# Eight of sixty-four gradient stores cut into pieces by rows, on two DMA queues

## The chip, the cores and the metric

The kernel runs on one core of a Trainium2 chip. Its time is the device time of that core in microseconds, as the median of several executions. Each execution is classed fast or slow (slow: over 1.5% above the fastest of the same kernel). The core has five engines that compute or issue (PE, DVE = VectorE, ACT = ScalarE, POOL = GpSimd, SP = SyncE) and 16 DMA engines, which move data between the chip's main memory (HBM) and the core's on-chip buffer (SBUF, 128 partitions). In the profile, SyncE's and ScalarE's transfers run on queues named hardware_dynamic, GpSimd's on one named software_dynamic.

## The reference

One decode step of attention beside a gated MLP, forward and backward. Only its sizes matter here: the K and V caches are 32 heads x 8192 x 128 in bf16, both are read, and the gradient of both is written.

```python
def _A_ref(x, k_cache, v_cache, wq, wo):
    ...
    scores = jnp.einsum("bhqd,bhkd->bhqk", q, k) * (Dh ** -0.5)
    p = _softmax(scores, axis=-1)
    o = jnp.einsum("bhqk,bhkd->bhqd", p, v)
    ...
_out0, _vjp = jax.vjp(_f, A_x, A_k_cache, A_v_cache, A_wq, A_wo, B_w1, B_w3, B_w2)
_grads = _vjp(grad_out)
```

That is 64 loads and 64 stores of 2 MB each, 268 of the 304 MB that the kernel moves.

## The kernel before

Each head of K or V is one tile of 128 partitions x 8192 elements: a row of 16 KB in each partition. The gradient overwrites the tile in place (`outer`), one store writes it out, and only then does a later load reuse the tile. All of these transfers go by SyncE, in program order.

```python
    kc = A_k_cache.rearrange("b h (p j) d -> (b h) p (j d)", p=P)      # P = 128
    dvc = out_3.rearrange("b h (p j) d -> (b h) p (j d)", p=P)
    ...
    def fifo(out_, in_):
        nc.sync.dma_start(out_, in_)
    ...
    def load_next():
        if not pending or len(free_slots) < lag[0]:
            return
        kind, h = pending.pop(0)
        t = free_slots.pop(0)
        fifo(t[:], (kc if kind == "K" else vc)[h])
        kv_tiles[(kind, h)] = t
    ...
    def store(kind, h):
        t = kv_tiles.pop((kind, h))
        if kind == "K":
            hd.pop(h)
        fifo((dkc if kind == "K" else dvc)[h], t[:])
        free_slots.append(t)
        load_next()
    ...
    def outers_a(h):
        outer_v(h, 0, J // 2)
        outer_v(h, J // 2, J)
        store("V", h)
        outer_k(h, 0, J // 2)
    ...
    # the last four small stores: 3, 2, 4 and 1 rows of 256 B
    for dst, r0, cuts in ((out_0, 0, (0, 3, 5)), (out_1, NC, (0, 4, 5))):
        for lo, hi in zip(cuts, cuts[1:]):
            nc.scalar.dma_start(...[lo:hi, :], fin_bf[r0 + lo:r0 + hi, :])
```

GpSimd's queue carries only weight traffic (`nc.gpsimd.dma_start` of pieces of 80 KB to 1.9 MB).

## Time and profile before

| | before |
|---|---|
| median | 737.14 us (736.62 to 739.97, the 3 runs taken before the prediction) |
| profiled span | 735.9 us |
| PE / DVE / ACT / POOL busy | 87 / 61 / 55 / 4% |
| one 16 KB row on a DMA engine, median and mean (packet records) | 611 and 620 ns |

From the page of the kernel before: the DMA busy share in 40 equal slices of the span (9 is 90% or more), what was moved in each, and the queues (q1 is SyncE's, q0 GpSimd's).

```profile
span 735.9 us, 14854 instructions
...
DMA  9999999999999999999999999999999999999993
GB/s 338 401 409 421 425 430 423 391 413 410 428 420 423 428 427 426 417 426 428 430 417 425 430 427 426 419 431 425 427 419 427 428 428 429 425 429 429 424 391 150
...
q1 hardware_dynamic: 21328, 276.39, 89.3%
q0 software_dynamic: 5728, 26.30, 8.9%
```

The table by windows of the kernel before; the last three columns are PE's granted clock, the DMA share and GB/s.

```profile
core 0: us, PE busy (x) PEld busy (x) DVE busy (x) ACT busy (x) POOL busy (x), PEclk, DMA share, GB/s
...
260.00:700.00 440.00, 410.47 (x3891) 295.45 (x3891) 277.16 (x424) 261.57 (x533) 15.55 (x19) 0.94 1.01 426
```

The DMA engines are full, and they move 426 GB/s. That is what bounds the kernel: 303.97 MB in rows of 16 KB per 611 ns on 16 engines is about 709 us.

SyncE's waits in the kernel before (what it waited for: us in total, times, longest).

```profile
SPq L101 <- DMA out_dram<-kv: 364.1, 44, 16.8
SPq L101 <- DVE kv L430: 174.0, 26, 11.0
...
SPq L822 <- DMA out_dram<-fin_bf: 11.6, 1, 11.6
SPq L822 <- DMA out_dram<-wq_g: 9.1, 1, 9.1
```

And the timeline near the end of the kernel before: the last gradient work on DVE, the last K store, the last small stores (start, duration).

```profile
707.98 4.49 DVE L430 TENSOR_TENSOR kv<-qd,U 128x4096 bf16<-128x4096 bf16 x2
...
712.50 0.33 SPq L101 DMA_DIRECT2D out_dram<-kv  x1
...
723.38 1.43 ACTq L796 DMA_DIRECT2D out_dram<-fin_bf  x4
```

The last work on DVE ends at 723.4 us, the last small stores are issued by 724.8, and the span ends at 735.9. The packet records of the trace (one record for each packet: queue, size, start, duration; no engine number) show that all DMA engines but one are done 8.4 us before the last packet. In those 8.4 us one engine works alone. On SyncE's queue each of the 137 transfers raises its counter 16 times (2192 completion packets of 4 B), and the gap between the last raise and the one before it grows from 0.2 to 1.2 us (transfers landing at 280 to 320 us) to 3.2 to 5.3 (480 to 520), 6.0 to 6.5 (640 to 680) and 8.2 to 8.4 us (707 to 717). One engine falls behind steadily.

### The profile page before, as it was taken

The page shows a single profiled execution, that of the slowest core. Times are in us where ns is not written, and L with a number is a line of the kernel's source. Part 1 is how long each engine was busy: PE and PEld are TensorE (multiplying, and loading weights), DVE is VectorE, ACT ScalarE, POOL GpSimd, SP SyncE. Part 2 cuts the span into 40 slices and gives each one's busy share as a digit, 9 for nine tenths or more (in the row PEclk, how much of TensorE's full clock was granted, in tenths as well). Part 3 has the DMA queues.
Part 4 walks back from the last instruction along what each step waited for, and adds up shares of the span by engine and source line. Part 5 has one row for each costly group of instructions (what it writes and reads, how often), then busy time and mean ns, then how long its engine had stood idle before and what let it go on. Part 6 is the DMA issues. An engine that isn't in the chain of part 4 may idle for free.

```text
span 735.9 us, 14854 instructions
## 1 busy us (share of the span) xinstructions
PE 639.8 (87%) x6143; PEld 464.7 (63%) x6143; DVE 446.7 (61%) x745; ACT 402.5 (55%) x796; POOL 29.9 (4%) x45
## 2 busy tenths in 40 slices
PE   1999679999999999999999999999999999989950
PEld 1667457676667666766666666766666666666630
DVE  4057765666556666667656656676666655566482
ACT  1660646565656565665565655666565556655610
POOL 0010010000000000000000000000000000000000
PEclk9995799998999999999999999999999999989965
DMA  9999999999999999999999999999999999999993
GB/s 338 401 409 421 425 430 423 391 413 410 428 420 423 428 427 426 417 426 428 430 417 425 430 427 426 419 431 425 427 419 427 428 428 429 425 429 429 424 391 150
DMA packets 27432, 303.97 MB, mean 413 GB/s; under 512 B 2836, under 2 KB 4436, under 8 KB 10724
## 3 DMA queue, kind: packets, MB, share of 16 engines
q1 hardware_dynamic: 21328, 276.39, 89.3%
q0 software_dynamic: 5728, 26.30, 8.9%
q8 instruction: 48, 0.79, 0.4%
q10 hardware_dynamic: 308, 0.33, 0.1%
q14 instruction: 20, 0.16, 0.1%
HBM read 151.67 MB, written 151.34 MB: 412 GB/s over the span
## 4 chain that ended last, share of the span: by engine, by line
PE 64%; DMA 12%; DVE 10%; ACT 8%; issue 3%; ACTq 0%; SPq 0%; DVEq 0%
PE pT L293 27%; PE m L328 8%; PE m L423 7%; DMA kv<-in_A_k_cache_dram 7%; PE sA L312 6%; PE pT L398 5%; ACT KT L295 4%; DVE kv L430 4%; DMA kv<-in_A_v_cache_dram 4%; PE dA L312 2%; DVE side L239 2%; ACT KT L318 2%; DMA wo_g<-in_A_wo_dram 2%; PE gu_ps L507 1%; PE m L372 1%
## 5 line engine op out<-in xcount | busy, mean ns | idle before, releaser
L295 ACT COPY KT<-pT 128x512 f32<-128x512 f32 x512 | 292.0, 590 | 185.6 <-PE pT L293 100.9
L293 PE MATMUL pT<-ident_f,kv 128*128 128x128 f32 x2048 | 311.3, 291 | 5.9 <-DMA kv<-in_A_k_cache_dram 4.0
L293 PEld LDWEIGHTS pT<-ident_f,kv 128*128 128x128 f32 x2048 | 245.8, 153 | 49.8 <-PE pT L293 17.5
L430 DVE TENSOR_TENSOR kv<-qd,U 128x4096 bf16<-128x4096 bf16 x64 | 146.0, 2284 | 0.0
L430 DVE TENSOR_TENSOR kv<-qd,P 128x4096 bf16<-128x4096 bf16 x64 | 143.5, 2283 | 0.0
L328 PEld LDWEIGHTS m<-selc,KT 128*128 128x128 f32 x512 | 62.3, 192 | 49.5 <-ACT KT L318 44.8
L328 PE MATMUL m<-selc,KT 128*128 128x16 f32 x512 | 68.0, 265 | 29.3 <-ACT KT L318 29.2
L423 PEld LDWEIGHTS m<-masks,KT 128*128 128x128 f32 x512 | 65.0, 200 | 15.4 <-issue 15.4
L354 DVE TENSOR_REDUCE mrow<-m 128x1 f32<-128x64 f32 x32 | 7.2, 225 | 106.4 <-PE m L328 106.4
L423 PE MATMUL m<-masks,KT 128*128 128x1 f32 x512 | 70.2, 259 | 0.0
L312 PE MATMUL sA<-KT,qz 128*32 128x512 bf16 x512 | 56.0, 427 | 0.0
L401 ACT COPY KT<-pT 128x512 f32<-128x512 f32 x64 | 38.7, 605 | 28.9 <-PE pT L398 28.7
L312 PE MATMUL dA<-KT,qz 128*32 128x512 bf16 x512 | 53.6, 404 | 0.2 <-ACT KT L295 0.2
L387 DVE SCALAR_TENSOR_TENSOR U<-m,P 128x64 bf16<-128x64 f32 x32 | 7.4, 232 | 75.7 <-PE m L328 72.7
L312 PEld LDWEIGHTS <-qz 128*32 128x32 bf16 x1024 | 26.6, 93 | 41.4 <-issue 40.3
L398 PE MATMUL pT<-kv,U 128*32 128x512 bf16 x512 | 46.2, 497 | 0.9 <-DVE U L411 0.9
L398 PE MATMUL pT<-kv,P 128*32 128x512 bf16 x512 | 34.7, 387 | 0.0
L348 ACT CAST qd<-pT 128x256 bf16<-128x256 f32 x32 | 11.9, 372 | 41.4 <-DVE kv L430 32.7
L398 PEld LDWEIGHTS <-U 128*32 128x32 bf16 x512 | 15.9, 116 | 18.5 <-issue 11.9
L480 DVE SCALAR_TENSOR_TENSOR wq_g<-wq_g,side 128x512 bf16<-128x512 bf16 x40 | 27.3, 684 | 0.0
L361 DVE TENSOR_REDUCE negM<-m 128x1 f32<-128x128 f32 x32 | 9.3, 292 | 29.6 <-PE m L358 29.6
L239 DVE SCALAR_TENSOR_TENSOR side<-wo_g,g_bc 128x640 bf16<-128x640 bf16 x32 | 26.2, 820 | 1.6 <-DMA wo_g<-in_A_wo_dram 1.2
(144 smaller groups left out, 405.6 us busy)
## 6 DMA issues: line engine op xcount, KB each, us to landing
out_dram<-kv SPq DMA_DIRECT2D x64, 2048.0 KB, 28.8
kv<-in_A_k_cache_dram SPq DMA_DIRECT2D x32, 2048.0 KB, 25.6
kv<-in_A_v_cache_dram SPq DMA_DIRECT2D x32, 2048.0 KB, 25.8
out_dram<-wo_g POOLq DMA_DIRECT2D x8, 640.0 KB, 12.1
out_dram<-wq_g POOLq DMA_DIRECT2D x8, 640.0 KB, 13.1
wq_g<-in_A_wq_dram POOLq DMA_DIRECT2D x7, 640.0 KB, 14.0
wo_g<-in_A_wo_dram POOLq DMA_DIRECT2D x7, 640.0 KB, 19.7
kv<-in_B_w_dram SPq DMA_DIRECT2D x2, 1728.0 KB, 29.7
```

Of the source, the lines that this page charges most:

```text
L239: nc.vector.scalar_tensor_tensor(junk[:], G_["wo"][:, hh, :], 1.0, g_bc[:], ALU.mult, ALU.mult, accum_out=G_["do"][:, hh:hh + 1])
L293: nc.tensor.transpose(pT[:, k * P:(k + 1) * P], W3[:, 4 * c + k, :], ident_f[:])
L295: nc.scalar.copy(KT[:].rearrange("p k w -> p (k w)"), pT[:])
L312: nc.tensor.matmul(S_[kind][q:q + QW, :], lhsT=S_["qz"][:, o:o + QW], rhs=KTb[:, par, :], start=(c0 == 0), stop=(c0 == NCH - 2), skip_grou ...
L318: nc.scalar.copy(XS[:].rearrange("p k w -> p (k w)"), S_.pop(kind)[:])
L328: nc.tensor.matmul(S_["m"][:, b0:b0 + J].rearrange("p (c k t) -> p k c t", k=4, t=2)[:, k, :, :], lhsT=XS[:, k, :], rhs=selc[:].rearrange( ...
L348: nc.scalar.copy(qd[:].rearrange("p a d -> p (a d)"), hd[h].pop("ps_r"))
L398: nc.tensor.matmul(X[q:q + QW, :], lhsT=pair[:, 4 * i:4 * i + QW, 0], rhs=W[:, N4 * i:N4 * (i + 1)], start=(i < 4), stop=(i >= J // 4 - 4) ...
L401: nc.scalar.copy(XS[:].rearrange("p k w -> p (k w)"), X[:])
L423: nc.tensor.matmul(S_["m"][:, OC + a:OC + a + 1], lhsT=XS[:, r, :], rhs=mask4[:, r:r + 1], start=False, stop=(r == 3), skip_group_check=True)
L430: nc.vector.tensor_tensor(dst[:, lo * DH:hi * DH].rearrange("p (j a b) -> p j a b", a=DH // 2, b=2), vec.rearrange("p (a b) -> p a b", b=2 ...
L480: nc.vector.scalar_tensor_tensor(wq_g[:, ci, :], wq_g[:, ci, :], 1.0, dqb, ALU.mult, ALU.mult, accum_out=dxa[:, ci, g:g + 1])
```

## The change

The intent is to take one 16 KB row from the late engine, held to be engine 4, in eight V stores (heads 9, 12, ... 30). GpSimd's 5-row piece was meant for engines 0 to 4 and its 11 rows for engines 5 to 15.

No packet record names an engine, so the numbers are names. As far as packets could be followed (three stores of the changed kernel, SyncE's packets in two of them; see e9), 0 to 4 are the five engines that carry the 512 B packets of a store, 0 to 3 those of them with SyncE's 4-row and 1-row packets, and 4 is the one without.

```diff
-        fifo((dkc if kind == "K" else dvc)[h], t[:])
+        dst = (dkc if kind == "K" else dvc)[h]
+        if kind == "V" and h >= 8 and h % 3 == 0:
+            R = P - 16
+            CT = 2 * P
+            fifo(dst[0:R], t[0:R])
+            nc.gpsimd.dma_start(dst[R:R + 5, 0:CT], t[R:R + 5, 0:CT])
+            nc.gpsimd.dma_start(dst[R + 5:P], t[R + 5:P])
+            fifo(dst[R:R + 4, CT:], t[R:R + 4, CT:])
+            fifo(dst[R + 4:R + 5, CT:], t[R + 4:R + 5, CT:])
+        else:
+            fifo(dst, t[:])
```

## The prediction

> **What bounds the kernel now.** The DMA engines. The page's slices show DMA at 9 tenths in 39 of 40 slices; from 15 to 700 us the table by windows has DMA share 1.01 to 1.02 and 410 to 427 GB/s, against PE 87%, DVE 61%, ACT 55%. The packet records show 16 packets in flight at nearly every moment, and a 16 KB row takes 611 ns (median and 90th percentile 611 and 621). 304 MB over 16 engines at 16 KB per 611 ns is about 709 us, so only some 27 us of the span are not row traffic: about 11 us before the first bulk packets, and the end.
>
> The end is where the change aims. The last compute, by the timeline, is over at 723.4 us, yet the span is 735.9: SyncE's last waits are for DMA (small output store 11.6, query-weight gradient 9.1, K store 1.0 us). The packet records show why: all engines but one finish their last packet about 8.4 us before the last one. In those 8.4 us a single engine alternates 16 KB rows of the final K store with 4 KB pieces of the weight-gradient store, then lands alone. One engine is simply behind, and time is its finish. The four small last stores have 3, 2, 4 and 1 rows and put 256 B packets on 3, 2, 4 and 1 engines at once; none falls in the late engine's sequence. [...]
>
> **What the change does.** For 8 V stores: 112 rows on SyncE (7 per engine); 11 whole rows and a 5 x 512 B piece on GpSimd; the rest of the five rows on SyncE as 4 and 1. [...] SyncE's 4 rows go to 0 to 3, the single row to engine 0 (the one-row output store was one packet on one engine). So engine 4 does 7 rows instead of 8, engine 0 does 9.
>
> Removed from engine 4: 8 x 0.611 = 4.9 us. Added there: eight 512 B pieces and completion writes (256 B took 20 ns, a 4 B write 9 ns), about 0.4 us. Engine 0 gains 4.9 us, but was done at least 8 us before the late one, and several engines idle about 5 us near the end. Extra issues: 16 on SyncE at 0.34 us, hidden in over 600 us of its waits; 16 on GpSimd at 0.6 to 0.9 us, which is 4% busy. Compute unchanged.
>
> **On the critical path:** nearly all of it, since the late engine never idles: about -4.4 us, with some given back if engine 0 becomes last.
>
> **Prediction: 733.0 us**, 80% range 731.0 to 737.0. Faster by over 2%: 0.01; within 2%: 0.97; slower: 0.02.
>
> **Right if:** the last packet moves about 4 us closer to the others' finish; last compute stays within some 3 us; GpSimd's queue carries 88 rows of 16 KB; DMA share stays at 1.01 in mid-run; SyncE's waits at the end shrink. **Wrong if:** [...]the 11 rows start at engine 0 (no gain, about 737.5); the late engine is not 4; the single row is spread over 16 engines (slightly better, 732.5); GpSimd's pieces issue late behind its waits and delay the next load; engine 0 or another becomes the late one.

The sum came to -4.9 us + 0.4 us on engine 4, put down as about -4.4 us; 737.1 less that is 732.7 us, stated as 733.0. That engine 4 is the late one, and that it does 7 rows and engine 0 nine, stand as my assumptions. What the trace of the change does show is the number of engines of the small SyncE pieces: 2232 completion packets of 4 B on SyncE's queue are 137 x 16, as before, and five more for each of the eight stores, 4 for the 4-row piece and 1 for the single row.

## The result, and the profile after

The changed kernel took 767.79 us (median of 4 runs, 762.42 to 774.77, one of them slow), the kernel before 737.18 us (4 runs). The ratio of the fast runs is 1.0383, 95% interval 1.0317 to 1.0449: about 28 us slower. Here and below a ratio is the mean time of one kernel's fast runs over that of the other's in the same rounds, so not quite the ratio of the medians. The prediction of 733.0 us was wrong, outside its range and in the opposite direction.

The profiled run of the change was its slowest (774.77 us), so it is used for where the time went; sizes come from the timed fast runs and from experiments whose profiles were fast.

The page of the changed kernel:

```profile
span 773.0 us, 14924 instructions
...
DMA  9999999999999999999999999999999999999946
GB/s 341 403 411 422 427 429 416 396 411 425 421 421 426 411 368 419 425 416 412 416 405 399 414 422 418 397 340 394 405 406 402 390 392 402 384 362 408 342 153 277
...
q1 hardware_dynamic: 21280, 274.93, 87.6%
q0 software_dynamic: 6240, 27.76, 9.4%
```

Its table by windows, the same stretch:

```profile
260.00:700.00 440.00, 395.39 (x3613) 284.08 (x3605) 257.29 (x397) 243.50 (x492) 22.40 (x32) 0.89 1.00 399
```

The DMA engines look as busy as before (share 1.00 against 1.01), yet they move 399 GB/s instead of 426. In the first 13 slices the two GB/s rows are alike within 4%; the first changed store is issued in slice 14 (at 262.6 us), and from there single slices fall as low as 340, the two at the end apart. A busy share that stays while GB/s falls means that packets take longer. The packet records agree: the mean 16 KB row on SyncE's queue went from 620 to 643 ns, and the 88 rows that now go by GpSimd took 1248 ns on average, up to about 3 us.

SyncE's waits, and the end of the timeline, in the changed kernel:

```profile
SPq L101 <- DMA out_dram<-kv: 431.7, 51, 17.4
SPq L101 <- DVE kv L430: 133.3, 18, 10.1
...
SPq L101 <- DMA out_dram<-fin_bf: 5.4, 1, 5.4
SPq L832 <- DMA out_dram<-wq_g: 4.9, 1, 4.9
```

```profile
739.21 4.49 DVE L430 TENSOR_TENSOR kv<-qd,U 128x4096 bf16<-128x4096 bf16 x2
...
754.65 2.47 ACTq L806 DMA_DIRECT2D out_dram<-fin_bf  x3
...
759.91 0.33 SPq L101 DMA_DIRECT2D out_dram<-kv  x1
```

The last gradient work now ends at 743.7 us instead of 712.5, because loads land later. There is also something new: the last K store is issued 16 us after its data are ready, where before it was issued at once.

From the packet records, the span can be split per engine. "Excess" is the time that rows of 15 KB and more took beyond 611 ns per 16 KB, summed and divided by 16; "idle" is the time in which an engine had no data packet (instruction fetches count as idle).

| us per engine | before | change | 112+16 rows (e2 below) |
|---|---|---|---|
| excess of large rows | 9.6 | 36.8 | 24.1 |
| idle | 14.8 | 24.2 | 21.7 |
| span of the profiled run | 735.9 | 773.0 | 757.6 |

27.2 of the 37.1 us are rows that take longer, 9.4 us are engines that run dry while others are held up. So the question is why rows take longer. The candidates were:

- **A, mismatch.** Rows of a piece that does not keep all 128 partitions take longer, because of the partitions that it reads. The packet records name neither engine nor partition, so this is not seen directly; e4 and e5 test it by the time of a row. How such rows come to be held up, no run shows.
- **B, count.** Five transfers instead of one: SyncE waits, completion counters.
- **C, GpSimd.** Its queue (software_dynamic) is slow for store pieces.
- **D, imbalance.** Engine 0 got extra rows and became the late one.

One more rival was not on my list. PE's granted clock was lower in the changed kernel (0.885 to 0.892 in its four runs, 0.903 to 0.920 in the runs of the kernel before). It can't be what lengthens the rows of such pieces: they are long in e4 too, where PE does nothing. And PE was idle for 45 of the 440 us in the window above, against 30 before. Whether the lower clock added to the loss was not tested.

### The profile page after: what moved, and what is told of

The parts are those of the page before. It is cut to its first block, busy times and chain, and to the rows that moved or that the text cites. A ratio compares the mean times of both kernels' runs of the same rounds, so it can differ in the third digit from the quotient of the medians.

```text
span 773.0 us, 14924 instructions
## 1 busy us (share of the span) xinstructions
PE 654.1 (85%) x6143; PEld 474.8 (61%) x6143; DVE 446.9 (58%) x745; ACT 404.9 (52%) x796; POOL 38.7 (5%) x61
## 4 chain that ended last, share of the span: by engine, by line
DMA 42%; PE 41%; DVE 6%; ACT 5%; issue 2%; SPq 0%; ACTq 0%; DVEq 0%
DMA out_dram<-kv 23%; DMA kv<-in_A_k_cache_dram 18%; PE pT L293 17%; PE m L328 5%; PE m L423 5%; PE pT L398 4%; PE sA L312 3%; ACT KT L295 3%; DVE kv L430 2%; PE dA L312 2%; DMA wo_g<-in_A_wo_dram 2%; ACT KT L318 1%; DVE side L239 1%; PE gu_ps L517 1%; ACT kv L590 1%
## 5 line engine op out<-in xcount | busy, mean ns | idle before, releaser
L293 PE MATMUL pT<-ident_f,kv 128*128 128x128 f32 x2048 | 318.8, 295 | 32.8 <-DMA kv<-in_A_k_cache_dram 27.7
L293 PEld LDWEIGHTS pT<-ident_f,kv 128*128 128x128 f32 x2048 | 251.1, 156 | 75.5 <-issue 37.3
L328 PEld LDWEIGHTS m<-selc,KT 128*128 128x128 f32 x512 | 65.8, 201 | 41.9 <-ACT KT L318 32.9
L328 PE MATMUL m<-selc,KT 128*128 128x16 f32 x512 | 71.7, 273 | 19.7 <-ACT KT L318 19.5
L398 PE MATMUL pT<-kv,U 128*32 128x512 bf16 x512 | 42.4, 462 | 0.9 <-DVE U L411 0.9
L398 PE MATMUL pT<-kv,P 128*32 128x512 bf16 x512 | 40.1, 437 | 0.0
## 6 DMA issues: line engine op xcount, KB each, us to landing
out_dram<-wq_g POOLq DMA_DIRECT2D x8, 640.0 KB, 14.5
```

The lines of the kernel that those rows point to most:

```text
L293: nc.tensor.transpose(pT[:, k * P:(k + 1) * P], W3[:, 4 * c + k, :], ident_f[:])
L328: nc.tensor.matmul(S_["m"][:, b0:b0 + J].rearrange("p (c k t) -> p k c t", k=4, t=2)[:, k, :, :], lhsT=XS[:, k, :], rhs=selc[:].rearrange( ...
L398: nc.tensor.matmul(X[q:q + QW, :], lhsT=pair[:, 4 * i:4 * i + QW, 0], rhs=W[:, N4 * i:N4 * (i + 1)], start=(i < 4), stop=(i >= J // 4 - 4) ...
```

## The experiments

### e1: five transfers on the same queues, but cut by columns

```diff
-            fifo(dst[0:R], t[0:R])
-            ...                                   # the four other row pieces
+            fifo(dst[:, 0:6528], t[:, 0:6528])
+            nc.gpsimd.dma_start(dst[:, 6528:6784], t[:, 6528:6784])
+            nc.gpsimd.dma_start(dst[:, 6784:7552], t[:, 6784:7552])
+            fifo(dst[:, 7552:7808], t[:, 7552:7808])
+            fifo(dst[:, 7808:], t[:, 7808:])
```

> The same eight V stores are cut into five transfers on the same two queues in the same order (SyncE, GpSimd, GpSimd, SyncE, SyncE), but by columns: each piece keeps all 128 partitions. Theory A (partition mismatch: a piece that does not span the 128 partitions [...]so rows take longer than 611 ns): no loss, 736 to 741 us, 16 KB-class rows stay at 611 to 620 ns. Theory B (more transfers: queue slots, completion counts, SyncE waits) and theory C (GpSimd's queue is slow for store pieces): about as slow as the change, 755 to 770 us.

Measured: 738.45 us (4 runs) against 737.33, ratio 1.002, interval 1.0005 to 1.0035. The excess of large rows is 9.9 us per engine, as before; its own 13 KB rows, too small for that count, take 492 ns, where 487 would be their share of 611. The table by windows of e1:

```profile
260.00:700.00 440.00, 407.05 (x3876) 292.78 (x3872) 275.27 (x421) 261.16 (x531) 24.36 (x35) 0.94 1.01 425
```

425 GB/s: nothing is lost. The number of transfers and GpSimd's queue together cost about 0.2%. B and C are out as causes of the 28 us.

### e2: 112 and 16 rows, both by SyncE

```diff
+            R = P - 16
+            fifo(dst[0:R], t[0:R])
+            fifo(dst[R:P], t[R:P])
```

> The eight V stores as 112 rows and 16 rows, both by SyncE, so 7 rows and 1 row for each of the 16 engines: no GpSimd, no imbalance, one more transfer. Theory A: still slow, 752 to 770 us, 16 KB rows with a mean well above 620 ns. Theory B (two more transfers than one cost little): under 745 us. Theory C (GpSimd) and theory D (engine 0 with 9 rows becomes the late one): no loss, about 737 us.

Measured: 764.99 us (4 runs, one slow), ratio 1.0413, interval 1.0352 to 1.0475. The whole loss is there with one extra transfer, no GpSimd, and 8 rows for every engine. D is out too. Its profile (a fast run; the last line is from the table by windows):

```profile
DMA  9999999999999999999999999999999999999974
GB/s 341 400 408 421 432 426 374 369 425 418 427 411 426 429 405 393 422 431 399 423 420 417 405 427 420 392 421 427 418 422 426 428 390 402 425 398 419 371 274 169
...
260.00:700.00 440.00, 403.77 (x3739) 290.19 (x3741) 268.35 (x411) 253.68 (x513) 15.59 (x19) 0.91 1.01 414
```

In or just after most of the slices in which one of the eight stores goes out, the row drops from about 425 to 390 or 405. (The dip in slices 7 and 8 comes before the first of them, at 265 us, and is not theirs.) In this fast run too, GB/s falls at an unchanged DMA share of 1.01.

### e3: 64 and 64 rows

```diff
+            R = P // 2
+            fifo(dst[0:R], t[0:R])
+            fifo(dst[R:P], t[R:P])
```

> The eight V stores as two halves of 64 partitions, both by SyncE, 4 rows per engine each: the dose test. Theory A [...]each row of these stores takes about twice 611 ns; 8 rows x 8 stores x 0.61 us = up to 39 us more, 755 to 780 us. Theories B, C, D: no loss beyond 2 us, because there is no GpSimd, equal rows per engine, and one more transfer per store.

Measured: 767.88 us (4 runs, one slow), ratio 1.037, interval 1.0301 to 1.0439. A holds, though the dose did not show: 64+64 is no slower than 112+16. Why was not shown. In e5 four such stores beside loads lost about 1.5 us more than whole ones; alone, in e4, four of 64 rows took 22.31 us, where half of the 21.36 us of whole ones would be 10.7.

### e4: the pieces by themselves

Wrong outputs. One tile is stored again and again, in groups of four transfers; a DVE write to the tile ends each group.

```python
    def mark():
        nc.vector.memset(t[:, 0:1024], 0.0)
    phases = [rows(nc.sync, 0, 128), rows(nc.sync, 0, 112), rows(nc.sync, 0, 96), rows(nc.sync, 0, 64),
              rows(nc.sync, 0, 32), rows(nc.sync, 112, 128), sw11, hw41, all5, cols5,
              rows(nc.gpsimd, 0, 128), rows(nc.gpsimd, 0, 112), rows(nc.sync, 0, 120)]
    for ph in phases:
        mark()
        for i in range(4):
            ph(...)          # a different head's output each time
```

> Wrong outputs on purpose: only stores from one tile, in thirteen groups of four, nothing else running, each group drained before the next. Theory A, mean time of one 16 KB row: whole 128 rows 611 ns; 112 rows about 730[...], 64 rows and 32 rows about 1220, the last 16 rows about 2440[...], GpSimd's 11 rows about 2280, SyncE's 4 rows about 2400; five column pieces like the whole. Theories B, C and D: all rows of SyncE's groups near 611 ns; C: only the groups issued by GpSimd are longer, the whole 128 rows by GpSimd included.

The timeline of e4, DVE only. The bracket of each line is what DVE waited for the group before it, so the first line shown belongs to the first group (four whole stores), and so on in the order of the list; the last group, 120 rows, has no line.

```profile
30.49 0.48 DVE L90 MEMSET kv<- 128x512 uint32 x1 [21.36 <-DMA out_dram<-kv]
56.31 0.48 DVE L90 MEMSET kv<- 128x512 uint32 x1 [25.34 <-DMA out_dram<-kv]
80.11 0.48 DVE L90 MEMSET kv<- 128x512 uint32 x1 [23.32 <-DMA out_dram<-kv]
102.91 0.48 DVE L90 MEMSET kv<- 128x512 uint32 x1 [22.31 <-DMA out_dram<-kv]
115.24 0.48 DVE L90 MEMSET kv<- 128x512 uint32 x1 [11.84 <-DMA out_dram<-kv]
127.47 0.48 DVE L90 MEMSET kv<- 128x512 uint32 x1 [11.75 <-DMA out_dram<-kv]
140.94 0.48 DVE L90 MEMSET kv<- 128x512 uint32 x1 [12.99 <-DMA out_dram<-kv]
153.08 0.48 DVE L90 MEMSET kv<- 128x512 uint32 x1 [11.65 <-DMA out_dram<-kv]
196.47 0.48 DVE L90 MEMSET kv<- 128x512 uint32 x1 [42.91 <-DMA out_dram<-kv]
216.12 0.48 DVE L90 MEMSET kv<- 128x512 uint32 x1 [19.16 <-DMA out_dram<-kv]
238.56 0.48 DVE L90 MEMSET kv<- 128x512 uint32 x1 [21.95 <-DMA out_dram<-kv]
264.75 0.48 DVE L90 MEMSET kv<- 128x512 uint32 x1 [25.71 <-DMA out_dram<-kv]
```

| group of four | bytes of one | DVE's wait | mean time of one large row |
|---|---|---|---|
| 128 rows, SyncE | 2.10 MB | 21.36 us | 618 ns |
| 112 rows, SyncE | 1.84 MB | 25.34 | 743 |
| 96 rows, SyncE | 1.57 MB | 23.32 | 798 |
| rows 0-63, SyncE | 1.05 MB | 22.31 | 1263 |
| rows 0-31, SyncE | 0.52 MB | 11.84 | 1267 |
| rows 112-127, SyncE | 0.26 MB | 11.75 | 2477 |
| GpSimd's 5-row and 11-row pieces | 0.18 MB | 12.99 | 1927 |
| SyncE's 4-row and 1-row pieces | 0.08 MB | 11.65 | 1944 |
| all five pieces of the change | 2.10 MB | 42.91 (spoilt in part) | 923 |
| five column pieces of e1, SyncE's three | 1.84 MB | 19.16 | 500 (13 KB) |
| 128 rows, GpSimd | 2.10 MB | 21.95 | 622 |
| 112 rows, GpSimd | 1.84 MB | 25.71 | 746 |
| 120 rows, SyncE | 1.97 MB | not shown | 861 |

A store of fewer bytes can take longer than the whole: 112 rows do (25.34 against 21.36 us). 64 rows take as long as 128 (22.31 us); 16 rows take four times 618 ns a row (2477). In both the 128-row and the 64-row groups some 15 rows are in flight on average (estimates from the table: 512 x 618 ns / 21.36 us = 14.8, 256 x 1263 ns / 22.31 us = 14.5), so it is the single row that takes longer. For SyncE's 112, 64, 32 and 16 rows the times are close to those expected under A (about 730, 1220, 1220 and 2440 ns). These expectations were 611 ns times a factor, and the factors (1.2, 2, 2 and 4) were my assumption, not shown by any earlier run; this run shows 1.2, 2.0, 2.1 and 4.0 times 618. The small pieces, expected from factors assumed in the same way, were quicker: 1927 against about 2280 ns and 1944 against about 2400. And 120 rows do not fit into the row of sizes: in the packet records 15 packets are in flight, and a row took 861 ns, longer than with 112 rows (743) or 96 (798). So A has the direction and several sizes, not every size.

A whole store is equally fast on GpSimd's queue, so C fails here as well. Alone, the change's five pieces cost (42.91 - 21.36) / 4 = 5.4 us more per store than one piece. A part of that is an accident: GpSimd's column pieces of the next group (1.05 MB) do not touch the columns that DVE writes, so nothing held them, and the packet records show them from 166 us on, beside this group. At 426 GB/s they are worth about 0.6 us per store (an estimate).

### e5: is it the buffer or the HBM side?

Groups of four as in e4 (again wrong outputs): three stores of 64 rows write the same number of rows, the first three groups differing in the partitions they read; then loads, and loads mixed with stores.

```python
    phases = [st(0, 0, 64), st(32, 0, 64), st(32, 32, 64), st(64, 0, 64), st(56, 0, 16),   # st(partition, HBM row, rows)
              ld(0, 0, 128), ld(0, 0, 112), ld(0, 0, 64), ld(32, 0, 64), ...
              both(ld(0, 0, 128), st(0, 0, 128)), both(ld(0, 0, 128), st(0, 0, 112)),
              both(ld(0, 0, 128), st(0, 0, 64))]
```

> Wrong outputs on purpose: groups of four transfers, each group drained before the next. Rival theories for the slow rows: A [...]against E (the order in which rows go to HBM). Stores of 64 rows to the same 64 HBM rows from partitions 0-63, 32-95 and 64-127: A[...]: about 1260, 611 and 1260 ns per row; E: the same time in all three. 16 rows from partitions 56-71[...]: about 2450. Loads: 128 rows 611; 112 rows about 740; 64 rows to 0-63 about 1260, to 32-95 about 611 under A. Loads of 128 rows mixed with stores of 128, 112, 64 rows[...].

The first group was spoilt: one of GpSimd's later groups had nothing to wait for and ran beside it; e4 has the same transfer clean (1263 ns). The timeline of e5 (the brackets of the 64-row stores from partitions 32-95 to HBM rows 0-63, from 32-95 to 32-95, from 64-127 to 0-63):

```profile
46.27 2.65 DVE L92 MEMSET kv<- 128x512 uint32 x5 [9.66 <-DMA out_dram<-kv]
58.60 2.65 DVE L92 MEMSET kv<- 128x512 uint32 x5 [9.68 <-DMA out_dram<-kv]
81.35 2.65 DVE L92 MEMSET kv<- 128x512 uint32 x5 [20.10 <-DMA out_dram<-kv]
```

Same rows of HBM, same number of rows: from partitions 32-95 a row takes 618 ns, from 64-127 1263 ns. Only the partitions differ, so the buffer side is the cause and the order in HBM is not. That partitions 32 to 95 would be the fast window was my assumption before the run. The run agrees with it, but what sets these partitions apart is not shown.

Loads behave alike. They pipeline, so the useful figure is the time from one landing to the next in DVE's timeline: about 4.9 us for 128 rows, 6.4 for 112, 4.9 to 5.9 for partitions 0-63, 2.45 for 32-95. Mixed with loads of 128 rows, stores of 112 rows cost less than alone: 43.1 us for four loads and four stores, where 60 rows per engine at 611 ns would be 36.7 us; whole stores in the same mix took 42.5 us for 64 rows (39.1). Stores of 64 rows took 34.2 us for 48 rows (29.3), so four of them lost about 1.5 us more than whole ones. e3 lost 28 us over sixteen such stores, about 1.8 us each. These groups thus show the cause, but not the size of the loss in the kernel.

### e6: rows 0-31, 32-95, 96-127

```diff
+            fifo(dst[0:32], t[0:32])
+            fifo(dst[32:96], t[32:96])
+            fifo(dst[96:P], t[96:P])
```

> The eight V stores in three pieces by SyncE: partitions 0-31, 32-95, 96-127. Theory A: the middle piece [...]costs nothing[...], so about half of the loss of the 64+64 split: 745 to 758 us. If it is the mere cutting into row blocks or the number of transfers (three against two): as slow as 64+64 or slower, 765 us and more.

Measured: 741.81 us (4 runs), ratio 1.0053, interval 1.0036 to 1.0069. Three row pieces cost 4 us where two cost 28. The direction is A's, and the mere cutting by rows or the number of transfers is refuted. The size is not A's: I expected half of e3's loss. In e4 rows 0-31 alone took 1267 ns a row; why the two outer pieces, of 32 rows each, cost so much less than half here was not tested.

### e7: only the 112 rows

Wrong output: 16 rows of these eight stores are never written.

```diff
+            fifo(dst[0:P - 16], t[0:P - 16])
```

> Wrong output on purpose: the eight V stores write only rows 0 to 111, nothing else; 2.1 MB less, worth 8 x 0.61 = 4.9 us by themselves. Theory A with the shares seen in the groups measured alone (rows of a 112-row store 743 ns, rows of the 16-row rest 2477 ns): the 112 rows carry about a third of the loss of 112+16, some 9 us, so about 741 us. If the small last piece alone were guilty: about 732 us. If the 112-row piece alone: about 760 us.

Measured: 749.5 us (4 runs, one of them at 760.43), ratio 1.0208, interval 1.0151 to 1.0264, unclear at 2%. This expectation missed: 2.1 MB less (4.9 us) and still 12 us more at the medians, so the 112-row pieces carry about 17 of e2's 28 to 30 us, and not a third. In the packet records of e7 two engines work alone for most of the last 8 us. Why two do was not shown. The row times measured in isolation (743 and 2477 ns) did not give the shares in the kernel.

### e8: the relief by columns

The main piece keeps all 128 partitions; of the last 1024 columns 120 rows go by GpSimd, between two dummy copies of 5 and 12 rows, meant to set which engine the 120 rows leave out. That they would was my assumption, not shown by any run.

```diff
+            C0 = KVN * 7 // 8
+            fifo(dst[:, 0:C0], t[:, 0:C0])
+            nc.gpsimd.dma_start(sh5[:], ident_bf[0:5, 0:16])
+            nc.gpsimd.dma_start(dst[8:P, C0:], t[8:P, C0:])
+            nc.gpsimd.dma_start(sh12[:], ident_bf[0:12, 0:16])
+            fifo(dst[0:4, C0:], t[0:4, C0:])
+            fifo(dst[4:8, C0:], t[4:8, C0:])
```

> The same relief of engine 4 with an eighth of the mismatched bytes: the eight V stores send 7/8 of the columns of all 128 partitions by SyncE; of the last 1024 columns, rows 8 to 127 go by GpSimd on 15 engines[...], rows 0-3 and 4-7 by SyncE on engines 0 to 3. Engine 4 again moves 16 KB less per store. Theory A: the loss shrinks to a few us at most and the relief of 4.9 us is nearly balanced or wins: 733 to 739 us. If the loss came from the number of transfers or from GpSimd's queue: 750 us or more.

Measured: 737.67 us (6 runs), ratio 0.9999, interval 0.9986 to 1.0012. With an eighth of the mismatched bytes the loss is gone, as A says. But the relief of 4.9 us did not appear either. The timeline of e8 shows the late last K store again:

```profile
709.23 4.49 DVE L430 TENSOR_TENSOR kv<-qd,U 128x4096 bf16<-128x4096 bf16 x2
...
727.66 0.33 SPq L101 DMA_DIRECT2D out_dram<-kv  x1
```

It is issued 14 us after its data. In the compiled program, which is not shown here, the last stores carry a wait on the completion of an earlier SyncE transfer (in the trace of the kernel before, each of the last three SyncE stores uses the semaphore of the SyncE transfer issued four before it, and is issued 0.3 to 0.7 us after that one's last raise), and two small pieces of head 30's store now stand between; the view of SyncE's waits says only that it waited for a DMA. My next theory (F) was that this ate the gain.

### e9, e10, e11, e12: away from the end

e9 is e8 on heads 6 to 27 (still eight stores), e10 is e9 with 2048 columns, e11 is e9 with its two dummy copies exchanged, e12 is the change itself on heads 6 to 27.

```diff
-        if kind == "V" and h >= 8 and h % 3 == 0:
+        if kind == "V" and 6 <= h < 30 and h % 3 == 0:
```

> The column relief of e8 on heads 6 to 27 instead of 9 to 30, still eight stores. Theory F: in e8 the relief was real but eaten at the end, because each SyncE store there waits for the completion of the one issued four before, and the two small pieces of head 30's store took two of these places, so the last K store was issued 14 us after its data were ready. Moved away from the end: the last K store is issued within 1 us of its data, and the time falls by most of 8 x 0.61 us: 733 us (732 to 735). If engine 4 was never the limit[...]: 737 us again.

> As e9 with the last 2048 columns instead of 1024: engine 4 sends two rows less per store, 9.8 us in all, twice the mismatched bytes. Theory A with F: the relief may exceed engine 4's lead of about 8 us over the next one, and mismatch costs more: 729 to 735 us; if mismatch at this dose eats the gain: 737 us or more.

> Control for which engine is late: e9 with its two dummy copies exchanged[...]; same pieces, same bytes, same number of transfers. If engine 4 alone is late: no gain, 737 to 739 us, against 733 in e9. If any unloading, or something else in e9, makes the gain: the same as e9.

> The change itself with its eight stores moved to heads 6 to 27, away from the end. Splits its loss into the part from mismatched partitions and the part from waits at the end (last K store issued 16 us after its data were ready). Theory A as the main cause: still 750 to 764 us. If the wait at the end were the main cause: under 742 us.

| | median us (before: 737.24) | ratio | 95% interval |
|---|---|---|---|
| e9 | 738.66 (6 runs) | 1.0014 | 0.9999 to 1.0029 |
| e10 | 738.85 (6 runs) | 1.0025 | 1.0006 to 1.0044 |
| e11 | 739.28 (6 runs) | 1.0035 | 1.0018 to 1.0051 |
| e12 | 774.15 (4 runs) | 1.0487 | 1.0439 to 1.0535 |

The timeline of e9 shows that the wait is cured:

```profile
708.25 4.49 DVE L430 TENSOR_TENSOR kv<-qd,U 128x4096 bf16<-128x4096 bf16 x2
...
712.77 0.33 SPq L101 DMA_DIRECT2D out_dram<-kv  x1
```

The time is not. So F falls: the late store was a consequence without a price of its own. e12 says the same of the change: away from the end it is not faster, but slower still, above the 750 to 764 us that I expected, and why it is slower than the change is open.

The packet records then gave the reason why e9 gained nothing. On GpSimd's queue the pieces have sizes of their own (512 B, 16 KB, 32 B, 4 KB), so that packets which follow each other without a gap on one engine can be strung together. In the changed kernel, for the three of the eight stores where all five 512 B packets could be followed, **each of the five engines that carry one also carries a 16 KB row of the same store**; six other engines carry a 16 KB row only. In two of these three stores SyncE's 4-row and 1-row packets could be followed as well: they fall on four of those five engines, and one of the four has two. So, by the names given above, the 5 rows went to engines 0 to 4 and the 11 rows to engines 0 to 10 (5 to 10 are the six others, 11 to 15 the rest). In the store at 479 us the late engine is the fifth, the one with a 512 B packet and no SyncE piece: engine 4. It is the late engine, and it did 7 + 1 = 8 rows, as before (counting the 112 rows as 7 for each engine: the store raises its counter 16 times, as a whole one does). Engine 0 did 10, engines 1 to 3 nine each, engines 11 to 15 seven. The change never took a row from engine 4.

In e9 and e11 GpSimd's 120 rows leave out one engine, and it carries none of the 32 B packets of the dummy copies, which fall on five and on twelve engines. The late engine carries its full share of the 120 rows in both. This fits 8 rows for each of 15 engines, the same 15 in e9 and e11; call the one left out 15. By this reading e8 to e11 all unloaded engine 15, and e11 was no control at all.

### e13, e14, e15: a relief that does reach engine 4

The pieces of 124 and of 4 rows were both meant for engines 0 to 3; that was my assumption. In e13's packet records at most four of their 768 B packets are in flight at once, leaving aside 0.1 us, so four engines fit; which four was not followed. The main piece keeps 128 partitions. If they are 0 to 3, all of engines 4 to 15 are unloaded alike, the late one among them.

```diff
+            C0 = KVN - 384                          # e14: 1024
+            fifo(dst[:, 0:C0], t[:, 0:C0])
+            fifo(dst[0:124, C0:], t[0:124, C0:])    # e15: 0:64
+            fifo(dst[124:P, C0:], t[124:P, C0:])    # e15: 64:128
```

> Eight V stores (heads 6 to 27): all 128 partitions by 7808 columns, then the last 384 columns as 124 rows and 4 rows[...]. Engine 4 sends 6 KB less per store, 1.8 us in all; engines 0 to 3 send 18 KB more, 5.5 us in all, within the 8 us by which the late engine trails the next one. If engine 4's load sets the time: about 1.5 us less than the control e15, so 735.5 to 736.5 us. If it doesn't: equal to the control.

> As e13 with 1024 columns: engine 4 sends 16 KB less per store (4.9 us in all), engines 0 to 3 send 48 KB more (14.7 us in all), more than the 8 us lead. If the time is the finish of the engine with the most work, one of engines 0 to 3 is now late: 741 to 747 us. If per-engine load doesn't set the time: about 738 us.

> Control without relief: the same three transfers per store with the last 384 columns as 64 and 64 rows, so all 16 engines share them evenly. A few small mismatched pieces: 737.5 to 739 us.

| | median us (before: 736.95) | ratio | 95% interval |
|---|---|---|---|
| e13, 1.8 us less on engine 4 | 735.35 (6 runs) | 0.9979 | 0.9961 to 0.9998 |
| e14, 4.9 us less on engine 4, 14.7 us more on 0 to 3 | 742.55 (4 runs) | 1.0091 | 1.0050 to 1.0132 |
| e15, control | 739.14 (6 runs) | 1.0020 | 0.9998 to 1.0042 |

All three moved in the expected direction; e14 fell into its range, e13 and e15 lie about 0.15 us outside theirs. The gap between the last engine and the next in the completion counters (transfers landing at 670 to 720 us) is 2.6 to 3.7 us in e13 against 6.5 to 8.2 in e15; it narrows also because engines 0 to 3 carry more. (e13's profiled run was its slowest, 738.15 us.) So the late engine's load does set the time, and unloading it by 1.8 us gains about that: 1.6 us at the medians against before, 3.8 against the control. Against before the gain is 0.2%, and its interval only just leaves out 1. That the late engine is 4 and no other of 4 to 15 rests on the packets followed above, not on e13. With e14, as its rise to 742.55 us suggests, the engines that take the load become the late ones.

## Why the prediction was wrong, point by point

- **"What bounds the kernel now: the DMA engines … one engine is simply behind, and time is its finish": right.** The trace of the change shows it in one store that was followed: of the five engines with a 512 B packet, the one without a SyncE piece, here called 4. e13 and e14, meant to load engines 0 to 3 and to unload all the others, move the time as that account says (735.35 and 742.55 us against 736.95). One number in that paragraph was misread: the "about 11 us before the first bulk packets" are mostly an offset of some 10 us between the clock of the packet records and the span. The first bulk packets start about 2 us into the span.
- **"Removed from engine 4: 8 x 0.611 = 4.9 us. Added there: … about 0.4 us": the step that failed, and the one that decided the result.** The sum charged each moved row 611 ns, whichever engine moved it and from whichever partitions. In e4 and e5 rows of whole stores and of stores from partitions 32-95 cost 618 ns. In other pieces they cost 743 (112 rows), 1927 (GpSimd's) and 1944 ns (SyncE's 4 and 1 rows). That term, left out, was worth about 28 us net; how it divides between these rows, other rows and landings held up was not separated. Shown by e1 (all five transfers, no mismatch: no loss), e2 (mismatch alone: the whole loss), e4 and e5.
- **"So engine 4 does 7 rows instead of 8": failed.** It needed the 11 rows to take engines 5 to 15. They took engines 0 to 10: in the three stores that could be followed, the five engines of the 512 B packets and six others. Engine 4 kept 8 rows, so not even the gain existed.
- **"The single row to engine 0": right** (40 packets of 15872 B, five per store; in the stores that could be followed, one engine with two). It made 10 rows, not the 9 that I wrote.
- **"Extra issues: 16 on SyncE …, 16 on GpSimd": right that they are cheap.** e1 has the same number and costs 0.2%.
- **"DMA share stays at 1.01 in mid-run": nearly true and useless.** It stayed at 1.00 while GB/s fell from 426 to 399. Busy share cannot tell a longer packet from more packets.
- **"GpSimd's queue carries 88 rows of 16 KB": right. "Last compute stays within some 3 us": wrong,** it ended over 30 us later.
- **"On the critical path: nearly all of it": right as mechanism,** as far as e13's small gain shows it, with a relief that arrives; for the change there was none.

What stays open: why engine 4 falls behind at all (instruction fetches do take a place among the 16 engines, 48 packets of 16 KB and 0.4% of the engines' time on the page of the kernel before, but the trace does not say on which), why e6 lost only 4 us, why 120 rows took 861 ns each, and why e12 is slower than the change.

## What to carry to other kernels

Cut a DMA between HBM and the on-chip buffer by columns, not by partitions: pieces that kept all 128 partitions cost little more than the whole (e1: 0.2%). Four stores of 112 partitions took longer than four whole ones (25.34 against 21.36 us), and four of 16 took more than half of that time for an eighth of the bytes (11.75 us). When DMA share is full, watch GB/s and the time of one packet, because a slower packet looks as busy as a fast one (here share 1.00 against 1.01 at 399 against 426 GB/s). Before counting on which engine a transfer lands, check it in the trace by packet sizes, and give every such plan a control that moves the same bytes without the effect.
